# Fused decode step: w2 products on two instead of four tiles, and the larger part of wq as the first transfer

## Chip, cores, metric

The kernel runs on one core of a Trainium2 chip. The metric is the time of one execution on the device in microseconds (us). "Span" is the part of it that the profile covers. In profiles PE is the matrix engine and PEld its loading of weights, DVE the vector engine, ACT the scalar engine, POOL a general-purpose one, and SP the engine that issues most transfers. A packet is one piece of a transfer, as the profile lists it, on one of the core's 16 transfer engines; a transfer has landed when all its packets have.

## The reference, cut

Two independent branches read the same input `x` (8 rows of 576) and are mixed by a gate:

```python
q = x @ wq                      # 576 x 4096, 32 heads of 128
p = softmax(q . k * Dh**-0.5)   # last 2048 keys of 16 KV heads
a = (p . v) @ wo                # 4096 x 576
h = gelu(layernorm(x) @ w1 + b1)            # 576 x 4608
b = h @ w2 + b2                             # 4608 x 576
g = sigmoid((x * gate_w).sum(-1))
out = g * a + (1 - g) * b
```

All data are bfloat16. K and V (64 MiB each in the window) dominate the 154 MB that must be read.

## The kernel before

A small planner lists every operation with its dependencies, orders each engine's instructions, and emits waits on semaphores. A dependency in `deps` is a wait; `after` only fixes the order of issue. All large transfers go through the queue of SP in this order: wq, w1, then K and V units, wo, and at the end w2 in four chunks, the last of them in three pieces.

The first transfers, the 64-row remainder of wq ahead of its main part:

```python
d_wqr = dma("sp", ... wq_r, A_wq[512:576, :] ..., "wq", 64 * 8192)                    # 128 rows of 4 KB
d_wqm = dma("sp", ... wq_m, A_wq[0:512, :] ..., "wq", 512 * 8192, after=[d_wqr])      # 128 rows of 32 KB
dwq = [d_wqm, d_wqr]                                                                  # the q product waits for both
d_w1m = dma("sp", ..., "w1", 512 * F * 2, after=[d_wqm])
```

The sums of the output. Each product has only 8 output rows, and the kernel puts it on a column tile of 32 (`tile_position`). The output's 576 columns are two halves (`j`), and with `split=2` successive products go to tiles 0 and 1, then 2 and 3; with `split=1` all go to tiles 0 and 1:

```python
class AccGroup:
    def __init__(self, name, mms, deps, cost, after=(), prio=0, split=2):
        def fn(e):
            for i, (lhsT, rhs) in enumerate(grp.mms):
                for j in range(NJ):                      # NJ = 2 halves of 288 columns
                    c = 64 * (i % split) + 32 * j
                    e.matmul(ps[c:c + 8, BK_ACC, 0:JN], lhsT, rhs[:, JN*j:JN*j+JN], ..., tile_position=(0, c))
...
def m2_chunk(ci):                                        # one chunk of w2: 9 rows of products, 18 matmuls
    cuts = [0, 4, 8, 9] if ci == FC - 1 else [0, FJ]
    for n, (j0, j1) in enumerate(zip(cuts, cuts[1:])):
        d = dma("sp", w2_fn, ...)
        ops.append(AccGroup("m2_%d_%d" % (ci, n), mms, [o_hT, d], ..., split=1 if ci == FC - 1 else 2).op)
        if ci == FC - 1 and n == 0:                      # copy of the second pair of tiles, on ACT
            odd = [g_.op for g_ in acc_groups if g_.split == 2]
            add("act", ... activation(out=accs[0:40, :], in_=ps[64:104, BK_ACC, 0:JN], Copy), deps=odd + ...)
...
o_fin = add("dve", ... out_sb = ps[0:40, BK_ACC] + accs ..., deps=acc_ops + o_ac)
```

## Time and profile before

| | |
|---|---|
| time, median of the first 3 readings | 366.93 us (366.67 to 367.24) |
| span of the profile | 365.7 us |
| transfers: share of 16 engines / mean rate | 98.6% / 423 GB/s |
| busiest compute engine | PE, 65% |
| last two w2 pieces landed; last ten products | 362.31 and 362.65 us; 362.35 to 363.71 us |

Eight of the last ten products read the last piece but one, two the last. They start when the last piece but one has landed; this landing, 362.31 us here, is what "last landing" means below. In a timeline row the columns are start, duration, engine, line, operation, output and input, count, and in brackets the engine's idle time just before with what ended it. L555 is the matmul of `AccGroup`, L807 the copy on ACT, L826 the final addition. PEclk is the clock granted to the array as a share of full speed. The rows themselves are in the prediction.

### The profile page before, as it was taken

Reading aid. Unit: us, or ns where it says so; the run is one execution under the profiler, and the core shown is the slowest. Engines: PE = TensorE matmul, PEld = TensorE weight load, DVE = VectorE, ACT = ScalarE, POOL = GpSimd, SP = SyncE. Lnnn points to the kernel's source line nnn. Section 1 sums busy time; section 2 is a strip of 40 time slices with the busy share of each in tenths; the row PEclk is TensorE's granted clock in tenths of the full one; section 3 lists DMA queues with packets and bytes.
Section 4 is the critical chain, followed back from the end, with each engine's and each line's share of the span. In section 5 each row is a group of like instructions: output and inputs, shape, how many; then the busy total and the mean of one; then the engine's idle time right before and its main releaser. Section 6 shows DMA issues by size and latency. Waiting matters only on the chain.

```text
span 365.7 us, 3979 instructions
## 1 busy us (share of the span) xinstructions
PE 239.5 (65%) x1679; PEld 114.4 (31%) x1679; DVE 226.5 (62%) x340; ACT 22.3 (6%) x53; POOL 17.4 (5%) x80
## 2 busy tenths in 40 slices
PE   0269684838498948274959294838959397297666
PEld 0159331312143414121524132214414133143232
DVE  4700995675999280759974452689790739974321
ACT  1010000000000000000100000001000000010000
POOL 4021000001000000010000000000000000000000
PEclk9999998778599969596998678676978698878885
DMA  9999999999999999999999999999999999999994
GB/s 386 440 412 432 410 448 430 430 442 409 453 409 454 405 446 419 425 439 428 444 418 446 418 455 412 456 407 452 407 452 409 455 399 434 429 429 428 429 426 184
DMA packets 9546, 154.58 MB, mean 423 GB/s; under 512 B 1036, under 2 KB 1204, under 8 KB 2744
## 3 DMA queue, kind: packets, MB, share of 16 engines
q1 hardware_dynamic: 9472, 154.29, 98.6%
q8 instruction: 13, 0.21, 0.2%
q10 hardware_dynamic: 56, 0.03, 0.0%
q14 instruction: 5, 0.04, 0.0%
HBM read 154.31 MB, written 0.01 MB: 422 GB/s over the span
## 4 chain that ended last, share of the span: by engine, by line
DMA 63%; DVE 26%; PE 8%; issue 1%; SPq 0%; DVEq 0%
DMA arena<-in_A_k_cache_dram 54%; DVE arena L666 19%; DMA arena<-in_A_v_cache_dram 5%; PE ps L711 4%; PE ps L678 4%; DMA arena<-in_B_w_dram 4%; DVE arena L639 3%; DVE arena L597 1%; DVE arena L761 1%; DVE arena L631 1%; DVE arena L600 0%; PE ps L555 0%; DVE arena L606 0%; DVE arena L614 0%; PE ps L612 0%
## 5 line engine op out<-in xcount | busy, mean ns | idle before, releaser
L666 DVE STREAM_TRANSPOSE arena<-arena 128x4096 f32<-128x4096 f32 x32 | 140.7, 4424 | 84.8 <-DMA arena<-in_A_k_cache_dram 84.3
L678 PE MATMUL ps<-arena 128*32 128x512 bf16 x512 | 139.7, 435 | 63.0 <-DVE arena L666 63.0
L678 PEld LDWEIGHTS ps<-arena 128*32 128x32 bf16 x512 | 51.6, 104 | 143.7 <-DVE arena L666 68.0
L711 PE MATMUL ps<-arena 128*32 128x512 bf16 x512 | 62.1, 456 | 23.1 <-DVE arena L602 18.7
L711 PEld LDWEIGHTS ps<-arena 128*32 128x32 bf16 x512 | 25.3, 110 | 50.0 <-issue 32.1
L639 DVE STREAM_TRANSPOSE arena<-arena 128x512 bf16<-128x512 bf16 x32 | 30.8, 1020 | 0.0
L728 PE MATMUL ps<-arena 128*128 128x16 f32 x128 | 16.9, 264 | 5.6 <-ACT arena L722 3.9
L761 DVE COPY arena<-arena 32x4 bf16<-32x4 bf16 (+1 forms) x80 | 12.9, 161 | 11.7 <-POOL arena L749 9.6
L728 PEld LDWEIGHTS ps<-arena 128*128 128x128 f32 x128 | 15.5, 191 | 11.9 <-ACT arena L722 9.6
L722 ACT ACTIVATE arena<-ps 128x512 f32<-128x512 f32 x16 | 9.6, 597 | 149.8 <-PE ps L711 149.8
L749 POOL TENSOR_TENSOR arena<-arena 128x8 bf16<-128x8 f32 x30 | 5.8, 230 | 230.0 <-ACT arena L738 230.0
L555 PE MATMUL ps<-arena 128*8 128x288 bf16 (+1 forms) x140 | 10.5, 365 | 4.5 <-DMA arena<-in_B_w_dram 3.0
L510 PE MATMUL ps<-arena 128*128 128x8 bf16 x144 | 10.9, 201 | 2.6 <-DMA arena<-in_B_w_dram 2.6
L597 DVE TENSOR_REDUCE arena<-ps 128x1 f32<-128x512 f32 x8 | 5.5, 692 | 11.1 <-PE ps L678 11.0
L608 ACT ACTIVATE arena<-ps,arena 128x512 bf16<-128x512 f32 x8 | 5.5, 687 | 105.9 <-DVE arena L606 105.9
L510 PEld LDWEIGHTS ps<-arena 128*128 128x128 bf16 x144 | 10.8, 159 | 3.1 <-DMA arena<-in_B_w_dram 3.1
L659 POOL TENSOR_TENSOR arena<-arena 128x32 bf16<-128x32 bf16 x32 | 6.4, 239 | 86.1 <-PE ps L678 77.0
L612 PE MATMUL ps<-arena 128*128 128x32 f32 x16 | 3.7, 314 | 8.8 <-DVE arena L611 8.8
L631 DVE TENSOR_SCALAR arena<-arena 128x512 bf16<-128x512 bf16 x32 | 9.0, 324 | 0.0
L425 PE MATMUL ps<-arena 8*128 8x8 bf16 x8 | 0.6, 171 | 11.0 <-DVE arena L398 7.0
L555 PEld LDWEIGHTS ps<-arena 128*8 128x8 bf16 (+1 forms) x140 | 4.3, 98 | 9.8 <-DMA arena<-in_B_w_dram 5.0
L512 PE MATMUL ps<-arena 128*128 128x8 bf16 x36 | 7.2, 201 | 0.0
(84 smaller groups left out, 77.7 us busy)
## 6 DMA issues: line engine op xcount, KB each, us to landing
arena<-in_A_k_cache_dram SPq DMA_DIRECT2D x16, 4096.0 KB, 25.1
arena<-in_A_v_cache_dram SPq DMA_DIRECT2D x32, 2048.0 KB, 24.4
arena<-in_B_w_dram SPq DMA_DIRECT2D x1, 4608.0 KB, 23.9
arena<-in_A_wo_dram SPq DMA_DIRECT2D x4, 1152.0 KB, 10.0
arena<-in_A_wq_dram SPq DMA_DIRECT2D x1, 4096.0 KB, 13.4
arena<-in_B_w_dram SPq DMA_DIRECT2D x3, 1296.0 KB, 18.9
arena<-in_B_w_dram SPq DMA_DIRECT2D x3, 576.0 KB, 13.3
arena<-in_A_wq_dram SPq DMA_DIRECT2D x1, 512.0 KB, 3.6
```

Source lines behind the costliest of these rows:

```text
L510: ins = e.matmul(out_, lhsT, yT[:, kt, :], start=(kt == 0), stop=False)
L512: ins = e.matmul(out_, lhsT, yT[:, 4 + c // 2, :], start=False, stop=True)
L555: ins = e.matmul(ps[c:c + 8, BK_ACC, 0:JN], lhsT, rhs[:, JN * j:JN * j + JN], start=False, stop=True, skip_group_check=True, tile_position ...
L597: mx = add("dve", lambda e: e.tensor_reduce(out=k(MX), in_=ps[:, bank, :], axis=AXL.X, op=ALU.max), deps=[qk_done[g]], name="mx%d" % g, co ...
L631: return e.tensor_scalar(out=dst, in0=view("Pd").rearrange("p (s n) -> p s n", s=2), scalar1=amask[:, a:a + 1], scalar2=None, op0=ALU.mult)
L639: return e.transpose(dst, src)
L666: tr = add("dve", (lambda h=h, kb=kb: lambda e: e.transpose(bass.AP(arena_f, offset=foffs("KT") + kb * SE // 2, ap=[[AST // 2, 128], [4, 1 ...
L678: mm = e.matmul(ps[32 * c:32 * c + 32, 2 * (G % 2) + nb, :], qb[:, G % 2, n, 2 * h + ee, :], rhs, start=(h == 0 and t == 0), stop=(h == 1 ...
L711: mm = e.matmul(ps[c:c + 32, bk, :], PT[:, g % 2, 512 * q + 32 * t:512 * q + 32 * t + 32], slot(s)[:, 512 * t:512 * t + 512], start=(t < 2 ...
L722: u_ev[item] = add("act", lambda e: e.activation(out=EV[:, item % 2, :], in_=ps[:, bk, :].rearrange("p (r d j) -> p r j d", r=4, j=4), fun ...
L728: mm = e.matmul(ps[:, BK_S, OC + 16 * (item % 2):OC + 16 * (item % 2) + 16], EV[:, item % 2, 128 * r:128 * r + 128], i2[:, r, :, :].rearra ...
L761: return [add("dve", (lambda j=j, q=q: lambda e: e.tensor_copy(oT[32 * q:32 * q + 32, ch, j, bs], oN[32 * j:32 * j + 32, q, ch, bs]))(), d ...
```

## The change

Two edits with separate intents. The large transfer goes first, so that the engines have much to do from the first moment. And all w2 products use the first pair of tiles, so that the ACT copy of the second pair needs to wait only for the projection and the bias.

```diff
-        d_wqr = dma("sp", ... wq_r ..., "wq", 64 * 8192, name="d_wqr")
-        d_wqm = dma("sp", ... wq_m ..., "wq", 512 * 8192, name="d_wqm", after=[d_wqr])
+        d_wqm = dma("sp", ... wq_m ..., "wq", 512 * 8192, name="d_wqm")
+        d_wqr = dma("sp", ... wq_r ..., "wq", 64 * 8192, name="d_wqr", after=[d_wqm])
...
-        d_w1m = dma(... after=[d_wqm])
+        d_w1m = dma(... after=[d_wqr])
...
-                ops.append(AccGroup(..., split=1 if ci == FC - 1 else 2).op)
+                ops.append(AccGroup(..., split=1).op)
```

More of the change, by code (lines that the diff above doesn't have):

```diff
@@ L387, in build_kernel @@
         db = [d_b1]
-        d_wqr = dma("sp", lambda e: e.dma_start(wq_r, A_wq[512:576, :].rearrange("k (s c) -> (k s) c", s=2)), "wq", 64 * 8192, name="d_wqr")
-        d_wqm = dma("sp", lambda e: e.dma_start(wq_m.rearrange("p t c -> p (t c)"), A_wq[0:512, :].rearrange("(p t) c -> p (t c)", t=4)), "wq", 512 * 8192, name="d_wqm", after=[d_wqr])
+        d_wqm = dma("sp", lambda e: e.dma_start(wq_m.rearrange("p t c -> p (t c)"), A_wq[0:512, :].rearrange("(p t) c -> p (t c)", t=4)), "wq", 512 * 8192, name="d_wqm")
+        d_wqr = dma("sp", lambda e: e.dma_start(wq_r, A_wq[512:576, :].rearrange("k (s c) -> (k s) c", s=2)), "wq", 64 * 8192, name="d_wqr", after=[d_wqm])
         dwq = [d_wqm, d_wqr]
-        d_w1m = dma("sp", lambda e: e.dma_start(w1_m.rearrange("p t c -> p (t c)"), B_w1[0:512, :].rearrange("(p t) c -> p (t c)", t=4)), "w1", 512 * F * 2, name="d_w1m", after=[d_wqm])
+        d_w1m = dma("sp", lambda e: e.dma_start(w1_m.rearrange("p t c -> p (t c)"), B_w1[0:512, :].rearrange("(p t) c -> p (t c)", t=4)), "w1", 512 * F * 2, name="d_w1m", after=[d_wqr])
         d_w1r = dma("sp", lambda e: e.dma_start(w1_r, B_w1[512:576, :].rearrange("k (s c) -> (k s) c", s=2)), "w1", 64 * F * 2, name="d_w1r", after=[d_w1m])
@@ L802, in m2_chunk @@
                 mms = [(hT[:, FJ * ci + j, :], dst[:, j * D:(j + 1) * D]) for j in range(j0, j1)]
-                ops.append(AccGroup("m2_%d_%d" % (ci, n), mms, [o_hT, d], cost=0.16 * (j1 - j0), after=o_m2[-1:], split=1 if ci == FC - 1 else 2).op)
+                ops.append(AccGroup("m2_%d_%d" % (ci, n), mms, [o_hT, d], cost=0.16 * (j1 - j0), after=o_m2[-1:], split=1).op)
                 o_m2.append(ops[-1])
```

## The prediction

Cut marks stand where a clause rested on a rule that no trace of this case shows. The sum: -0.2 us for the order of wq and +0.22 us for the pair of tiles, together about 0, so 366.9 us.

> **What bounds the kernel now.** I read the page first (busy shares, forty slices, queues), then the chain that ended last, then the queue of transfers in its first microseconds, and last the timeline of the final 12 us, because the change touches only the start and the end. The page:
>
> ```profile
> span 365.7 us, 3979 instructions
> ...
> PE 239.5 (65%) x1679; PEld 114.4 (31%) x1679; DVE 226.5 (62%) x340; ACT 22.3 (6%) x53; POOL 17.4 (5%) x80
> ...
> DMA  9999999999999999999999999999999999999994
> GB/s 386 440 412 432 410 448 430 430 442 409 453 409 454 405 446 419 425 439 428 444 418 446 418 455 412 456 407 452 407 452 409 455 399 434 429 429 428 429 426 184
> ...
> q1 hardware_dynamic: 9472, 154.29, 98.6%
> ...
> DMA 63%; DVE 26%; PE 8%; issue 1%; SPq 0%; DVEq 0%
> ```
>
> The reader is to see that the transfers are never idle: 39 of 40 slices show nine tenths or more, and one queue holds the 16 engines for 98.6% of the span. No compute engine is above 65%. The chain names DVE for 26%, but while those transposes run the transfers go on at full rate, so DVE there only hands out buffers; it sets no time as long as the queue behind it is not empty. In 30 us stretches from 60 to 358 us the same rate is found ten times (422 to 439 GB/s, mean about 430). The time is therefore: some start until the first byte, 154.3 MB at about 430 GB/s (359 us), and a tail after the last byte. The change can act only through start, rate, an empty queue, or tail.
>
> The start, as the queue shows it in half microseconds (packets, MB, share of 16 engines) at 1.0, 1.5, 2.0 and 2.5 us; nothing moves before 1.0:
>
> ```profile
> q1 hardware_dynamic: 27, 0.11, 97.1%
> ...
> q1 hardware_dynamic: 38, 0.16, 76.3%
> ...
> q1 hardware_dynamic: 31, 0.13, 62.2%
> ...
> q1 hardware_dynamic: 56, 0.55, 268.5%
> ```
>
> These are mostly the 128 packets of 4 KB of the small wq transfer: 27 + 38 + 31 = 96 by 2.5 us, the rest soon after. The shares of 76% and 62% are the only holes that I find outside the tail. (A share over 100% comes from booking a 32 KB packet wholly in one slot.) Packets of nearly the same size (4.6 KB, of w2) in full stream, at 358 to 359 us, have no such holes:
>
> ```profile
> DMA packets 90, 0.41 MB, mean 409 GB/s; under 512 B 11, under 2 KB 13, under 8 KB 81
> ```
>
> The work that waits for the start, and the SP queue's next issues:
>
> ```profile
> 10.03 0.30 DVE L398 COPY arena<-arena 8x64 bf16<-8x64 bf16 x2 [4.12 <-DMA arena<-in_gate_w_dram]
> ...
> 18.02 0.27 PE L472 MATMUL ps<-arena 128*128 128x8 bf16 x4
> ```
>
> ```profile
> 2.36 20.66 SPq L649 DMA_DIRECT2D arena<-in_A_k_cache_dram  x2
> ```
>
> The q product starts at 18.02 although wq landed at 0.44 + 13.4 = 13.84 us; it waits in PE order for the y transposes at 17.30, which hang on the small gate rows. The second K unit is issued when the q product is done, about 22.5 us; the first K unit lands at 36.52, so there are some 12 us of queued work at that moment.
>
> The tail, on the timeline:
>
> ```profile
> 353.74 0.78 PE L555 MATMUL ps<-arena 128*8 128x288 bf16 x18
> ...
> 356.35 2.32 PE L555 MATMUL ps<-arena 128*8 128x288 bf16 x34 [1.84 <-DMA arena<-in_B_w_dram]
> 359.44 0.81 PEld L555 LDWEIGHTS ps<-arena 128*8 128x8 bf16 x18 [1.32 <-DMA arena<-in_B_w_dram]
> 359.45 2.50 PE L555 MATMUL ps<-arena 128*8 128x288 bf16 x26 [0.77 <-DMA arena<-in_B_w_dram]
> ...
> 360.86 0.41 ACT L807 ACTIVATE arena<-ps 40x288 f32<-40x288 f32 x1 [8.16 <-PE ps L555]
> 362.35 0.81 PEld L555 LDWEIGHTS ps<-arena 128*8 128x8 bf16 x10 [0.95 <-DMA arena<-in_B_w_dram]
> 362.35 1.36 PE L555 MATMUL ps<-arena 128*8 128x288 bf16 x10 [0.40 <-DMA arena<-in_B_w_dram]
> 363.76 0.45 DVE L826 TENSOR_TENSOR arena<-ps,arena 40x288 bf16<-40x288 f32 x1 [6.58 <-PE ps L555]
> ```
>
> The 18 at 353.74 are chunk 0 of w2, the 34 are chunk 1 and the last 16 products of the projection, the 26 are chunk 2 and the first piece of chunk 3, and the 10 are its last two pieces. PE waits only 0.40 us for the last landing: it is almost caught up with the transfers. That small slack is what the change can eat.
>
> [...]at the same slow clock chunk 2 does 18 products on four tiles in about 1.36 us (359.45 to 360.81), and the last pieces need the same 1.36 us for 10 products on two tiles. [...]the groups here start 0.24 us apart (362.55, 362.79, 363.03) at a granted clock of 0.50[...]. [...]here the clock stays at 0.50 from about 355 us to the end although PE is busy for 0.5 of each half microsecond from 359.5 to 361.5[...]. [...]the gate rows, issued at 1.27 us, are used only at 10.03, behind 32 KB packets.
>
> **The change part by part.**
>
> *Order of wq.* Bytes, packets, buffers and the semaphore's final count stay; the q product waits for both parts before and after. Moved: the 128 packets of 4 KB go from the cold start into the stream. At the start 0.524 MB takes from 1.0 to about 2.7 us, 1.7 us. In the stream, at the 409 GB/s above, it takes 0.524 MB / 409 GB/s = 1.28 us. That is 0.4 us, of which about 0.13 us is the slower first packet[...] (97% busy with 27 packets is 0.29 us for each; at 76% with 38 it is 0.16). That leaves -0.3 us at best. As a check, the first 36 us after the first byte moved 15.27 MB, 424 GB/s against 430 later, which is 0.5 us behind and bounds the gain. I book -0.2 us. It lies on the path, because the stream has no later hole to swallow it.
>
> *First pair of tiles for chunks 0 to 2.* No product is removed. 54 products lose half their parallelism: a chunk has 18 products, which are 4.5 groups of four before and 9 pairs after. At 0.24 us between starts: chunk 1 from 356.35 is done issuing at 358.5 (9 x 0.24 = 2.16), the 16 projection products (4 groups, 0.96) at 359.45, just when chunk 2 lands at 359.44. Chunk 2 then issues until 359.45 + 2.16 = 361.6. The first piece of chunk 3 (4 pairs, 0.96) until 362.57. Before, the last 10 products began at 362.35 on their landing; now they begin at 362.57. So +0.22 us on the path.
>
> *The copy on ACT* no longer waits for chunks 0 to 2, only for the projection and bias, so it can run at about 359.7 instead of 360.86. It ended at 361.27 and its reader starts at 363.76: 2.5 us of slack, worth nothing.
>
> *Sum:* -0.2 + 0.22 = about 0. Time 366.93 + 0.0 = 366.9 us.
>
> **The rivals.**
>
> *The clock wakes.* PE is busier in the tail, so the granted clock may go up. Then pairs start 0.12 us apart; chunk 2 ends before the last landing and the last 5 pairs take 0.6 us less: 366.1 with the start's gain. For it: chunk 0 runs at full clock, 18 products in 0.78 us. Against it: the clock falls at 355 and the busy stretch after 359.5 does not raise it. One in six.
>
> *The reorder delays the small transfers.* x and the gate rows now share the engines with 32 KB packets from the start, so the normalization may begin 1 to 2 us later. With 12 us of queue at the second K issue nothing is lost: 366.9 still. Only a delay over 10 us would empty the queue.
>
> *Small packets cost the same wherever they are.* Then the start gives nothing and the tail's +0.22 remains: 367.1 to 367.2. If the projection also slips past 359.45, 367.3.
>
> *PE's delay is hidden.* The last landing could be what ends it, with PE catching up, if the first piece of chunk 3 is issued earlier than I read: 366.6 to 366.7.
>
> **Range and chances.** The readings of before spread over 0.57 us (366.67 to 367.24), and my terms are each below 0.7 us. I predict 366.9 us, and 366.2 to 367.6 should hold it 8 times in 10. Two per cent is 7.3 us, ten times any term here; it would take an emptied queue or a broken order. Faster by over 2%: 0.01; within 2%: 0.98; slower: 0.01.
>
> **What would show it.** Start: packets of 32 KB from 1.0 us, and the landing of the first K unit at about 36.3 instead of 36.52; if it is unchanged, the first step fails. Tail: 18 products of chunk 2 taking about 2.3 us instead of 1.36, and PE's wait before the last 10 products gone (they start later than their landing); if a wait on the transfer remains there, the second step is wrong. Clock: 0.50 to the end; 1.00 there means the first rival. The copy on ACT about a microsecond earlier with no effect. What would make it all wrong is a slice of the transfer row below nine tenths in the middle, which would mean that the queue ran empty.

## The result, and the profile after

The changed kernel took 366.61 us (median of 4 readings, 366.52 to 366.66), against 366.93 us. A ratio here is the mean time of one kernel's fast runs over that of the other's in the same rounds, so it is not quite the ratio of the medians: 0.9991, with a 95% interval of 0.9974 to 1.0008. By their times the two kernels cannot be told apart.

Each engine has as many instructions as before, and the page looks alike. After:

```profile
span 365.2 us, 3979 instructions
...
PE 240.5 (66%) x1679; PEld 115.6 (32%) x1679; DVE 226.3 (62%) x340; ACT 22.4 (6%) x53; POOL 17.4 (5%) x80
...
q1 hardware_dynamic: 9472, 154.29, 98.8%
...
DMA 63%; DVE 26%; PE 8%; issue 1%; SPq 0%; DVEq 0%
```

The difference of half a microsecond in the span must be looked for at its two ends. The start first, in the queue's rows (packets, MB, share of 16 engines) after, in the stretches 1.0 to 1.5, 3.0 to 3.5 and 4 to 5 us:

```profile
q1 hardware_dynamic: 15, 0.49, 373.5%
...
q1 hardware_dynamic: 13, 0.43, 199.1%
...
q1 hardware_dynamic: 16, 0.52, 121.3%
```

A packet is booked in the stretch in which it starts, so its duration can be worked out: 373.5% of 16 engines for 0.5 us is 29.9 engine-microseconds over 15 packets, 1.99 us each. In the last row it is 1.213 x 16 / 16 = 1.21 us for the same 32 KB. The holes of before (62.2% from 2.0 to 2.5 us) are gone, but the first packets are slow after the change too, and as 32 KB packets they took 1.99 us each instead of 1.21. All of wq had landed at 13.73 us (before 13.81), but the main part of w1 at 25.29 (before 25.16), and the first K unit at 2.21 + 34.44 = 36.65 (before 36.52). Nothing was won at the start; 0.1 us was lost.

The tail, on the timeline after:

```profile
353.94 1.27 PE L555 MATMUL ps<-arena 128*8 128x288 bf16 x18
...
356.55 5.14 PE L555 MATMUL ps<-arena 128*8 128x288 bf16 x60 [1.33 <-DMA arena<-in_B_w_dram]
...
359.89 0.41 ACT L807 ACTIVATE arena<-ps 40x288 f32<-40x288 f32 x1 [6.99 <-PE ps L555]
...
362.45 0.46 PEld L555 LDWEIGHTS ps<-arena 128*8 128x8 bf16 x10 [1.07 <-DMA arena<-in_B_w_dram]
362.45 0.78 PE L555 MATMUL ps<-arena 128*8 128x288 bf16 x10 [0.76 <-DMA arena<-in_B_w_dram]
363.27 0.45 DVE L826 TENSOR_TENSOR arena<-ps,arena 40x288 bf16<-40x288 f32 x1 [5.88 <-PE ps L555]
```

Chunk 1, the projection, chunk 2 and the first piece of chunk 3 are now one stretch of 5.14 us without a gap; before, they were two stretches of 2.32 and 2.50 us with 0.77 us between. The last ten products start 0.10 us later, but take 0.78 us instead of 1.36. So in this profile the end of the products moves by +0.10 - 0.58 = -0.48 us, which is the half microsecond of the span. What changed there is the clock. In half microseconds, before (columns: length, busy time of PE, PE's weight loads, DVE, ACT, POOL, then granted clock, share of transfers, GB/s):

```profile
359.00:359.50 0.50, 0.05 (x4) 0.06 (x8) 0.00 (x0) 0.00 (x0) 0.00 (x0) 0.50 0.97 389
...
362.50:363.00 0.50, 0.50 (x6) 0.27 (x4) 0.00 (x0) 0.00 (x0) 0.00 (x0) 0.50 0.00 0
```

The same view after:

```profile
359.00:359.50 0.50, 0.50 (x10) 0.17 (x4) 0.00 (x0) 0.00 (x0) 0.00 (x0) 0.50 0.95 376
359.50:360.00 0.50, 0.50 (x10) 0.23 (x8) 0.00 (x0) 0.11 (x1) 0.00 (x0) 0.68 0.73 295
...
362.50:363.00 0.50, 0.50 (x10) 0.31 (x10) 0.00 (x0) 0.00 (x0) 0.00 (x0) 1.00 0.00 0
```

After, the clock goes from 0.50 to 1.00 at about 359.8 us (0.68 is the mean of that half microsecond), some 3.3 us into the unbroken stretch. Before, PE was idle for most of 359.0 to 359.5, and the clock stayed at half to the end.

### The profile page after: what moved, and what is told of

It is laid out like the page before. It is cut to its first block, busy times and chain, and to the rows that moved or that the text cites. A ratio compares the mean times of both kernels' runs of the same rounds, so it can differ in the third digit from the quotient of the medians.

```text
span 365.2 us, 3979 instructions
## 1 busy us (share of the span) xinstructions
PE 240.5 (66%) x1679; PEld 115.6 (32%) x1679; DVE 226.3 (62%) x340; ACT 22.4 (6%) x53; POOL 17.4 (5%) x80
## 4 chain that ended last, share of the span: by engine, by line
DMA 63%; DVE 26%; PE 8%; issue 1%; SPq 0%; DVEq 0%
DMA arena<-in_A_k_cache_dram 54%; DVE arena L666 20%; PE ps L678 6%; DMA arena<-in_A_v_cache_dram 5%; DMA arena<-in_B_w_dram 4%; DVE arena L639 3%; PE ps L711 2%; DVE arena L631 1%; DVE arena L597 1%; DVE arena L600 0%; DVE arena L606 0%; DVE arena L614 0%; PE ps L555 0%; DVE arena L611 0%; PE ps L612 0%
## 5 line engine op out<-in xcount | busy, mean ns | idle before, releaser
L555 PE MATMUL ps<-arena 128*8 128x288 bf16 (+1 forms) x140 | 11.6, 356 | 2.1 <-DMA arena<-in_B_w_dram 2.1
L555 PEld LDWEIGHTS ps<-arena 128*8 128x8 bf16 (+1 forms) x140 | 5.6, 97 | 7.3 <-DMA arena<-in_B_w_dram 3.5
```

The source lines that it names most:

```text
L555: ins = e.matmul(ps[c:c + 8, BK_ACC, 0:JN], lhsT, rhs[:, JN * j:JN * j + JN], start=False, stop=True, skip_group_check=True, tile_position ...
```

## The experiments

**Theory A:** fewer tiles make PE work longer without a gap, which gives the clock back before the last ten products; the order of wq gains nothing, because the first packets are slow at either size (4 KB: 0.29 against 0.16 us before; 32 KB: 1.99 against 1.21 us after). **Rivals:** B, the order brings the gain; C, the pair of tiles as such or the earlier copy on ACT brings it; D, the clock at the end is chance. The first four kernels ran in the same rounds on one chip (before: 366.87 us, 11 readings of 366.09 to 367.64).

**1. The order of wq alone** (`split` as before).

```diff
-  AccGroup(..., split=1).op)
+  AccGroup(..., split=1 if ci == FC - 1 else 2).op)     # on the changed kernel
```

> Only the order of the two wq transfers is changed. Theory A (the first packets on the idle engines are slow whatever their size, so the order gains nothing at the start): last w2 landing within 0.2 us of before, second wq part landing at about 13.7 us, first K unit at 36.5 to 36.8; time within 0.2 us of before in the mean, and the end still at a granted clock of 0.50 with the last ten products in about 1.36 us. Rival B (the reorder is what brings the gain, by 0.3 us): time lower by about 0.3 us with the landings 0.3 us earlier.

Measured: 367.81 us (367.31 to 368.18), ratio 1.0022 (1.0009 to 1.0035). Its last ten products on the timeline:

```profile
363.50 1.14 PE L555 MATMUL ps<-arena 128*8 128x288 bf16 x10 [0.27 <-DMA arena<-in_B_w_dram]
```

B falls. Theory A was right that there is no gain, and about the slow clock for most of the tail, but it had not foreseen a loss of 0.9 us. The start was as expected (all of wq landed at 13.70 us, the first K unit at 36.71), but the last landing, expected within 0.2 us of before, came 1.15 us later than before, at 363.46, which is more than the whole loss. Runs 6, 11 and 12 look at that again.

**2. The pair of tiles alone** (order of wq as before).

```diff
-  AccGroup(..., split=1 if ci == FC - 1 else 2).op)
+  AccGroup(..., split=1).op)                             # on the kernel before
```

> Only the products of w2 on the first pair of tiles. Theory A (longer unbroken PE work in the last 6 us brings the full clock back before the last ten products): all of the gain is here, 0.3 to 0.5 us below before; granted clock 1.00 after about 359 to 361 us and the last ten products in about 0.78 us. Rival B: no gain or a loss of 0.2 us, last ten products still 1.36 us and starting after their landing.

Measured: 366.36 us (366.26 to 366.62), ratio 0.9988 (0.9975 to 1.0001). The last ten products:

```profile
362.21 0.78 PE L555 MATMUL ps<-arena 128*8 128x288 bf16 x10 [0.93 <-DMA arena<-in_B_w_dram]
```

The gain is here, in the place and the size that A gives it, though the interval just reaches 1. But in this execution the clock was at 1.00 in every half microsecond from 354.0 to 363.5 us: it was not given back, as A has it, but not lost in this stretch.

**3. Four tiles as before, but PE's gaps filled.** Seven spare products whose result nobody reads: 4 after chunk 1 and the projection, 1 after chunk 2, 2 after the first piece of chunk 3. The order of wq is the old one.

```diff
+  FILLS = {(1, 0): 4, (2, 0): 1, (3, 0): 2}
+  for _ in range(FILLS.get((ci, n), 0)):
+      e.matmul(ps[0:8, 0, 0:JN], hT[:, 0, :], ones_bf[:, 0:JN], start=True, stop=True, tile_position=(0, 0))
```

> The kernel before, with four tiles for chunks 0 to 2, plus seven spare products whose result nobody reads, placed in PE's gaps: 4 after chunk 1 and the projection, 1 after chunk 2, 2 after the first piece of chunk 3. Theory A (it is PE's unbroken activity that counts, not the pair of tiles): the clock is 1.00 for the last ten products, which take about 0.78 us, and the time is 0.3 to 0.5 us below before. Rival C (the gain belongs to the pair of tiles itself or to the earlier copy on ACT): clock 0.50 at the end, time equal to before or up to 0.2 us above.

Measured: 366.29 us median of 6, four of them 366.16 to 366.31 and two of 367.31 and 367.65; ratio 0.9993 (0.9977 to 1.0009). In the profile, the clock reaches 1.00 at about 361.3 us, after 3.45 us of unbroken work from 357.86 us (the copy on ACT starts at 361.19). The half microsecond in which it rises, and the last ten:

```profile
361.00:361.50 0.50, 0.50 (x8) 0.29 (x6) 0.00 (x0) 0.31 (x1) 0.00 (x0) 0.69 0.33 131
...
362.11 0.78 PE L555 MATMUL ps<-arena 128*8 128x288 bf16 x10
```

This is the experiment that separates A from C: four tiles, the copy on ACT as late as ever, and the last ten products are as short as with the pair of tiles. Filled gaps, a clock of 1.00 for the last ten products and 0.78 us for them came together in this profile and again in that of run 12. The gain in time is only seen in four of six readings; no profile was taken of the two slow ones, so the interval does not confirm it.

**4. The changed kernel with the copy on ACT held back** to where it was.

```diff
-  odd = [g_.op for g_ in acc_groups if g_.split == 2]
+  odd = [g_.op for g_ in acc_groups[:-1]]
```

> The changed kernel, with the copy on ACT waiting for all earlier groups again, as before. Theory A: no effect, time as the changed kernel (366.5 to 366.7), copy about a microsecond later. Rival C (the earlier copy brings the gain): time back at 366.9.

Measured: 366.83 us (366.41 to 367.07), between the two values expected. The median does not decide; the timeline does:

```profile
360.94 0.41 ACT L807 ACTIVATE arena<-ps 40x288 f32<-40x288 f32 x1 [6.52 <-PE ps L555]
...
362.40 0.78 PE L555 MATMUL ps<-arena 128*8 128x288 bf16 x10 [0.74 <-DMA arena<-in_B_w_dram]
```

The copy is a microsecond later than in the changed kernel and still ends 1.8 us before the last ten products do; nothing waits for it. Its intended use is worth nothing here.

The next four ran on another chip (before: 366.88 us, 9 readings of 366.75 to 367.06).

**5. The kernel before again**, unchanged, for a second profile.

> The kernel before, unchanged, for a second profile. Theory A (gaps in PE's work keep the clock down at the end): granted clock 0.50 for the last ten products again, 1.2 to 1.4 us, last landing 362.0 to 362.5. Rival D (the clock at the end is chance[...]): it may as well be 1.00.

Measured: 366.83 us, one reading. The last ten products:

```profile
362.18 1.36 PE L555 MATMUL ps<-arena 128*8 128x288 bf16 x10 [0.36 <-DMA arena<-in_B_w_dram]
```

The same slow clock and the same 1.36 us.

**6. The order alone again**, unchanged, for a second profile.

> The kernel with the order of wq alone, for a second profile. If the late last landing of its first profile (363.46) belongs to the order, it is late again, above 363 us; if it was chance of one transfer engine, it is back at about 362.4 us. Clock at the end 0.50 under theory A.

Measured: 367.84 us, one reading, with the late landing once more:

```profile
363.25 1.30 PE L555 MATMUL ps<-arena 128*8 128x288 bf16 x10 [0.44 <-DMA arena<-in_B_w_dram]
```

It also shows a limit of theory A. PE had 3.29 us of unbroken work here (from 359.53 us, since the projection was late), and still the clock rose only at 364.36 us, too late for most of the last ten. It had fallen at 357.54, so 6.82 us lie between, twice 3.41. Half way, at 360.95, PE had been busy for 1.8 of the 3.41 us since the fall, and the clock stayed at 0.50. The same spacing is found elsewhere: in the traces of before and after each change of the clock lies a whole multiple of 3.41 us after the one before it, and fall and rise are 3.41 us apart in runs 3 and 10 and 6.83 us in run 1. Why the changes are spaced so is not shown.

**7. Smaller packets first.** On the changed kernel, the first MB of wq's main part is a transfer of its own with rows of 8 KB, then the rest with rows of 24 KB.

```diff
-  d_wqm = dma("sp", ... wq_m, A_wq[0:512] as (p t) c -> p (t c) ...)
+  d_wq0 = dma("sp", ... wq_m[:, 0, :],   A_wq4[:, 0, :] ...)
+  d_wqm = dma("sp", ... wq_m[:, 1:4, :], A_wq4[:, 1:4, :] ..., after=[d_wq0])
```

> The changed kernel, but the first MB of the main part of wq goes out as its own transfer with rows of 8 KB, then the rest in rows of 24 KB, then the remainder. If the size of the first packets on the cold engines is what makes the changed order fall behind (1.31 against 1.40 to 1.43 MB moved 4 us after the first packet), some 1.36 to 1.40 MB are moved by then and the time is 0.1 to 0.2 us below the changed kernel; if not, 1.31 MB and 366.6 us.

Measured: 366.51 us (366.11 to 366.85), ratio 0.9990 (0.9977 to 1.0004); 0.1 us below the changed kernel's first median and 0.6 below its later one (run 9), neither of them from the same rounds, so the expected gain in time is not settled. The queue's row from 1.0 to 1.5 us and the last ten products:

```profile
q1 hardware_dynamic: 15, 0.12, 125.8%
```

```profile
362.05 0.78 PE L555 MATMUL ps<-arena 128*8 128x288 bf16 x10 [0.72 <-DMA arena<-in_B_w_dram]
```

The first 8 KB packets take 1.258 x 8 / 15 = 0.67 us each; at 3.0 to 3.5 us they take 0.31. So the first packets were slow at all three sizes tried, 4 KB (0.29 against 0.16 us in the mean), 8 KB (0.67 against 0.31) and 32 KB (1.99 against 1.21), by 0.13, 0.36 and 0.78 us. From the packets of the traces, with each packet's bytes spread evenly over its duration, one can count what had been moved 4 us after the first packet: 1.40 to 1.43 MB with the small part first in five of six profiles (1.35 in the sixth, run 8), 1.31 to 1.34 MB in all seven with the 32 KB rows first, and 1.42 MB here. The difference of some 0.08 MB is 0.2 us of the stream (an estimate, at 430 GB/s). The landing of the first K unit agrees: 36.41 to 36.64 us in the six profiles of the old order, 36.65 to 36.82 in the seven with 32 KB rows first, 0.2 us later in the mean, and 36.41 here. The new order loses that; the prediction had it gain as much.

**8. Old order, pair of tiles, and gaps filled**, as the version that should be best.

```diff
+  FILLS = {(0, 0): 9, (1, 0): 4, (2, 0): 2, (3, 0): 3}   # and split=1 for all chunks
```

> The old order of wq, w2 on the first pair of tiles, and 18 spare products in PE's gaps (9 after chunk 0, 4 after chunk 1, 2 after chunk 2, 3 after the first piece of chunk 3). Theory A: the clock is 1.00 through the whole tail, last ten products 0.78 us, no PE delay behind the landings; time 366.1 to 366.4 us, as the kernel with the pair of tiles alone or up to 0.2 us less, below both kernels of the case. Rival: the spare products get in the way of the landings, 366.6 or more.

Measured: 366.52 us (366.25 to 367.41), ratio 0.9993 (0.9980 to 1.0005); the median lies between the two expectations. The profiled execution is the slow one of 367.41 us. The spare products (L811) are in the way of the last pieces:

```profile
362.38 0.77 PE L555 MATMUL ps<-arena 128*8 128x288 bf16 x6
...
363.23 0.29 PE L811 MATMUL ps<-arena 128*8 128x288 bf16 x1
363.24 0.89 PE L555 MATMUL ps<-arena 128*8 128x288 bf16 x8
```

The clock is at 1.00 from 354 us on, and still PE ran behind the landings from 359.07 us to the end. In that execution the last V products had been late as well (they ended at 353.9 us, before at 352.0), so all of the tail was pushed together. Filling more than is needed showed no gain; in this one execution the rival that was written down is right.

The last four ran together on a third chip, as a comparison of both parts in the same rounds (before: 366.93 us, 11 readings of 366.70 to 367.64).

**9. The changed kernel again.**

> The changed kernel, unchanged, in the same rounds as its two parts. Theory A: 366.5 to 366.7 us, full clock for the last ten products (0.78 us), last landing about 362.4 us.

Measured: 367.14 us (366.90 to 367.31), ratio 1.0004 (0.9992 to 1.0016): the expected clock, but not the expected time.

```profile
363.13 0.78 PE L555 MATMUL ps<-arena 128*8 128x288 bf16 x10 [1.40 <-DMA arena<-in_B_w_dram]
```

**10. The pair of tiles alone again.**

> The pair of tiles alone, old order of wq, again. Theory A: 366.3 to 366.5 us, 0.1 to 0.3 us below the changed kernel of the same rounds, because about 0.09 MB more are moved in the first 4 us; last ten products 0.78 us. If the two are equal, the order is neutral at the end although it is behind at the start.

Measured: 366.37 us (366.19 to 366.91), ratio 0.9984 (0.9971 to 0.9997), the expected time, but 0.6 us in the mean below the changed kernel of the same rounds (366.48 and 367.12), at least twice the expected distance.

```profile
362.86 0.78 PE L555 MATMUL ps<-arena 128*8 128x288 bf16 x10 [0.73 <-DMA arena<-in_B_w_dram]
```

**11. The order alone, a third time.**

> The order of wq alone, again. Its six earlier readings lay at 367.3 to 368.2 with a last landing at 363.2 to 363.5. If that belongs to this kernel, it is 0.6 to 1.0 us above before again, on whatever chip; if it was chance, 367.0 to 367.2 (0.1 to 0.3 above before).

Measured: 366.97 us median of 6, but from 366.33 to 368.01; ratio 1.0002 (0.9990 to 1.0015). The landing is early this time, so the loss of 0.9 us is not a fixed property of this kernel. The last ten products, and the half microsecond in which the clock falls:

```profile
362.33 1.37 PE L555 MATMUL ps<-arena 128*8 128x288 bf16 x10 [0.37 <-DMA arena<-in_B_w_dram]
```

```profile
360.50:361.00 0.50, 0.17 (x2) 0.09 (x4) 0.00 (x0) 0.18 (x1) 0.00 (x0) 0.85 0.50 205
```

Here the clock was full until 360.8 us. PE, quick on its four tiles, was busy for 1.44 of the 3.30 us before that (0.23 us of the half microsecond from 360.0, 0.17 of the next), and the clock fell ahead of the last ten products. That the short work lost the clock is not shown by this one profile.

**12. The order with four tiles and filled gaps** (run 3's seven spare products on run 1's kernel).

> The new order of wq, four tiles as before, plus the seven spare products of the earlier fill. If the late last landing comes with the new order on four tiles, it is there again (above 363 us) and the time is 367.0 or more although the clock is full at the end; if it does not belong to the order, the last landing is at about 362.4 us, and the time 366.5 to 366.7, as the changed kernel.

Measured: 366.88 us median of 6 (366.43 to 368.48), ratio 1.0002 (0.9987 to 1.0018). The clock is full for the last ten products, and the landing is late:

```profile
363.05 0.78 PE L555 MATMUL ps<-arena 128*8 128x288 bf16 x10
```

The expectation had tied a late landing to 367.0 us or more; the profiled execution has it with a time of 367.12 us, but the median of all six lies between the two cases that were written down. The run is inconclusive on whether the landing belongs to the order.

**All profiles together.** The last ten products take 0.78 us in all eight in which PE works on two tiles or with moderate filling (after, after again, split twice, fill, late copy, 8 KB first, order with fill), and 1.14 to 1.37 us in all five with four tiles and open gaps (before twice, the order alone three times). D, pure chance, falls: that would hardly part 13 profiles so cleanly. But a part of D stays, because the moments at which the clock changed differ between executions of one kernel (the order alone: it fell at 357.46 us in run 1 and at 360.85 in run 11). The full clock at the end came about in two ways. In four of the eight (after, split again, fill, order with fill) it had fallen by 357.9 us and came back in time, at 359.8, 359.9, 361.3 and 362.5 us; in the other four it was full in every half microsecond from 356.0 us until the last ten were done. Theory A spoke only of the first way. PE was busy for 96% of the 3.41 us before the clock came back in the changed kernel (356.40 to 359.82), and for 77% of a stretch as long in the kernel before (358.39 to 361.80) and 76% in its second profile (358.87 to 362.28), after which it stayed at half.

The busy share alone does not tell what the clock does: in the kernel before, PE was busy for 48% of the stretch from 337.91 to 341.32 us and the clock stayed full, and for 73% of that from 351.56 to 354.98 and it fell. What else decides is not shown.

With two tiles or filled gaps the clock was full for the last ten products in eight of eight profiles, which makes it likely, not certain. Four tiles with open gaps did not have it for all of them in any of five. Run 8 is left out, since its ten were mixed with spare products.

The start of the last ten, which follows the last landing by 0.04 to 0.05 us, lies at 362.11 to 362.86 in the five profiles with the old order (mean 362.34) and at 362.33 to 363.50 in the seven with the new order of 32 KB rows first (mean 362.87). So the landing varies by over a microsecond between executions, twice the gain of the clock, and the new order is on the late side of it by 0.5 us in the mean, of which 0.2 us is the slower start. Where the rest comes from, and whether it is more than chance, is open: the two ranges overlap.

The order with the pair of tiles against the pair alone was 0.6 us slower in the same rounds (9 and 10); without it the loss was 0.8 us on one chip (1) and 0.05 us on another (11). In the rounds of 9 to 12 the pair of tiles gained 0.5 us with the old order and nothing with the new one (367.04 and 367.12 in the mean). Why is not shown: the changed kernel's profile has a late last landing and that of the order alone an early one, but only one execution of each was profiled. The best supported version is the pair of tiles with the old order: 366.36 and 366.37 us on two chips, about half a microsecond below before; one of its two intervals excludes 1, the other ends at 1.0001.

## Why the prediction was right or wrong

The time was right: 366.61 us, and 367.14 in the later rounds, inside 366.2 to 367.6. So was the reading that the transfers bound everything and only start and tail could move. But each of its two terms had the wrong sign; that two wrong terms again nearly cancelled is luck.

*"Order of wq", -0.2 us.* The step that failed is the cost of the first packets: the prediction subtracted 0.13 us for them (0.29 less 0.16 us, read off 4 KB packets; that it holds for any size was the estimate), and put the rest down to the small packets. The holes did go with the small packets, but at 32 KB the first packets took 1.99 instead of 1.21 us, a loss of 0.78 us and not 0.13. The measured term is +0.1 us at the landing of the first K unit in the pair of profiles, and +0.2 us over all profiles (run 7), there and in bytes moved after 4 us. The test that the prediction set itself (a first K landing at 36.3, else the step fails) came out at 36.65.

*"First pair of tiles", +0.22 us.* The counting of groups was right as long as the clock was slow: at a clock of 0.50, PE was still occupied by this work until after 359.5, and chunk 2 did follow with no gap. What failed is the step that held the clock at 0.50 to the end. It had argued from before, where a busy stretch after 359.5 raised nothing. That stretch was shorter: 2.50 us after 0.77 us of idle, and PE was busy for 77% of the 3.41 us from 358.39 to 361.80, against 96% before the rise in the changed kernel. The change itself removes that gap, as the prediction's own sum showed (chunk 1 and projection until 359.45, chunk 2 landing at 359.44). The rival "the clock wakes", given one in six, is what happened in the profile, and its size of 0.6 us for the last 5 pairs was right (1.36 - 0.78 = 0.58); its time of 366.1 us was not reached, as it counted on a gain at the start. The pair alone came out 0.5 us faster (run 2), not 0.22 slower. "PE's wait before the last 10 products gone" was wrong for the same reason: 0.76 us of wait were left.

*"The copy on ACT", nothing:* right, by the profile of run 4. *"The reorder delays the small transfers":* did not matter; the gate rows were used at 9.93 us instead of 10.03.

## What to carry to other kernels

Where PE mostly waits for transfers, look at the granted clock in the stretch that ends the kernel (on four tiles, run 11 lost the full clock at 360.8 us, and its last ten products took 1.37 us, against 0.78 in the eight profiles with the full clock), and when a change closes a gap of PE, ask whether it changes the clock. When a transfer is moved to the start, look for what the first packets of its own size cost there: a penalty of 0.13 us read off 4 KB packets was 0.78 us at 32 KB. And where two edits come together with a difference of a tenth of a per cent, run each alone, in the same rounds and on more than one chip: here the better kernel was one half of the change.
